# First attention of a block-sparse attention and FNet kernel: order written by hand, keys and queries turned two tokens at once, block sums on TensorE, a third value buffer

## Chip, cores, metric

The kernel runs on one core of one Trainium2 chip. The metric is device time in microseconds (us). The profile is that of one execution; its times count from the first instruction. Names of engines: PE is TensorE (PEld its weight loads), DVE is VectorE, ACT is ScalarE, POOL is GpSimd, SP is SyncE, which issues the transfers. PSUM is the memory that PE writes into, in banks of 512 fp32 columns on 128 partitions.

## What is computed

Four batches, eight heads, 768 tokens of 64 channels. Every query sees the keys closer than 16 tokens and, beside them, one summary for each of 24 blocks of 32 tokens: the maximum of the block's keys and the mean of its values. Then a mixing by Fourier transforms, a normalisation, and two dense layers (512 to 2048 to 512).

```python
k_sum = k.reshape(B, H, nb, block, D).max(axis=3)      # block = 32
v_sum = v.reshape(B, H, nb, block, D).mean(axis=3)
scores_l = scale * np.matmul(q, k.transpose(0, 1, 3, 2))
mask_l = np.abs(pos[:, None] - pos[None, :]) < window  # window = 16
scores_s = scale * np.einsum('bhsd,bhnd->bhsn', q, k_sum) + np.log(block)
...
out = np.matmul(softmax(concat(masked scores_l, scores_s)), concat(v, v_sum))
x = heads of out side by side, [B, S, 512]
u = x + np.real(fft(fft(x, axis=1), axis=2))
un = (u - mean(u)) / np.sqrt(var(u) + 1e-06)
result = u + np.maximum(un @ w_ch1, 0) @ w_ch2
```

Since exp(s + log 32) times a mean is exp(s) times a sum, the kernel works with block sums of the values.

## The kernel before

The program is one long pipeline. Attention of the next batch is interleaved with the dense layers of the current one, so that PE seldom rests; only batch 0's attention (the "first attention") has nothing to run beside, and it stands at the start. It is built differently from the others ("wide").

**The first attention** works on four pairs of heads, g = 0 to 3; a pair's two heads e = 0, 1 share the 128 partitions, 64 channels each. Its steps for a pair:

- `load` (L579) brings keys and queries, `kn` and `qn`, from memory with tokens on partitions, three tokens a partition. `prepare` (L703) turns them: 24 matmuls with the identity (L718), which the profile counts as 48 records, write channels onto partitions in PSUM (`qk`), and ACT copies (L719) bring them to `kt` and `qt`. `key_maxima` (L699, L700 on DVE) reduces `kt` to the 24 block maxima `km`.
- `wide_scores` (L740) takes queries in six blocks of 64, in two halves of three blocks. A block needs 96 keys (64 and 16 on each side). Local scores (L750) fill rows 0 to 95 of a score bank `sc`, the scores of the maxima (L754) rows 96 to 127. ACT takes exponentials (L756) into `p`, DVE multiplies by the mask `wide` (through the helper at L571).
- `block_sums` (L614) and `add_blocks` (L605): two transfers of 768 KB each bring the values of four heads once more, to the tile `words` as 96 blocks by 2048 numbers, and DVE adds halves five times (L571) to get the block sums `vbs`. `sum_values` (L762) spreads them with a selection matrix `sel` on PE (L767, into `vs`) and copies them to rows 96 to 127 of the value buffer `vw`, once for each query block (L769, DVE for pairs 0 and 3, ACT for 1 and 2).
- `load_values` (L664) brings the local values to rows 0 to 95 of `vw` in six transfers a pair; there are two such buffers, so pair 2 uses pair 0's after pair 0's values have been multiplied.
- `wide_values` (L772): PE multiplies (L777, into `av`), DVE takes reciprocals of the row sums (L781) and writes the products to `x`.
- `fold_sequence` and `fold_halves` (L896, L901) add and subtract halves of `x`, for the Fourier tables; each needs `x` of a pair, or of two.

**What sets the order.** For PE and DVE the order within `first_attention` is that of the code, under `tc.manual_schedule`; ACT's order there, and everything behind the first attention, is set by a list scheduler, which goes by ready times that it estimates and by priorities. SP issues its transfers in the order of the code (`fetch`, L549) up to the hidden layer. A few transfers can be outstanding at a time, so an SP instruction waits until a slot or a buffer is free, and those behind it wait as well.

**Behind the first attention** come the Fourier tables (PE lines 1258, 1262, 1297, 1299), the normalisation (DVE and ACT lines 1276 to 1331, then PE transposes at L1353), and the first hidden layer (`hx`, `hy`, `hz` at PE line 1381; the names are the seven-product scheme's banks, joined on DVE with `tt` into `h`). The attention of batch 1 runs beside them: its keys and queries are turned by 128x128 transposes (L726) and copied in pieces of 64 rows (L729). The weights arrive as 64-bit floats and are converted to fp32 on DVE and ACT on the way, in the lines 1092 to 1116 (`words` is the raw data, `w` the result); a conversion has two short DVE steps (0.7 us), three longer ones (1.2 us), and one or two of ACT.

## Time and profile before

| | us |
|---|---|
| median of three runs | 787.74 |
| lowest, highest | 786.42, 788.77 |
| profiled execution, span from first to last instruction | 787.6 |
| PE busy in that span | 771.0 (98%) |
| DVE busy | 536.3 (68%) |
| ACT busy | 241.8 (31%) |
| first scores of pair 0 (PE line 750) | 7.97 |
| last reciprocal of the first attention (L781, pair 3) | 43.77 |
| first hidden-layer matmul (PE line 1381) | 85.94 |

The span is the profiled execution's own time as the profile gives it. In the views, a row gives the start in us, the length, the engine, the line, the operation, what it writes and reads, and how many instructions the row groups; in brackets stands how long the engine was idle before, and what released it. Matmuls of one group may overlap, so that the distance between starts says more than lengths.

### The profile page before, as it was taken

The page shows a single profiled execution, that of the slowest core. Times are in us where ns is not written, and L with a number is a line of the kernel's source. Part 1 is how long each engine was busy: PE and PEld are TensorE (multiplying, and loading weights), DVE is VectorE, ACT ScalarE, POOL GpSimd, SP SyncE. Part 2 cuts the span into 40 slices and gives each one's busy share as a digit, 9 for nine tenths or more (in the row PEclk, how much of TensorE's full clock was granted, in tenths as well). Part 3 has the DMA queues.
Part 4 walks back from the last instruction along what each step waited for, and adds up shares of the span by engine and source line. Part 5 has one row for each costly group of instructions (what it writes and reads, how often), then busy time and mean ns, then how long its engine had stood idle before and what let it go on. Part 6 is the DMA issues. An engine that isn't in the chain of part 4 may idle for free.

```text
span 787.6 us, 14943 instructions
## 1 busy us (share of the span) xinstructions
PE 771.0 (98%) x6076; PEld 582.2 (74%) x6076; DVE 536.3 (68%) x1121; ACT 241.8 (31%) x561; POOL 74.6 (9%) x99
## 2 busy tenths in 40 slices
PE   8999899999999999999999999999999999999997
PEld 5878455445579866688569876688659889889986
DVE  4899979697988647652577635463476987766762
ACT  3555557236535112100226112210126214204300
POOL 0000000000000020200120011300030004201500
PEclk9999999999999999999999999999999999999999
DMA  8999785796966369996344159830614044204001
GB/s 182 200 279 236 178 281 158 232 251 230 222 196 177 71 174 189 261 156 143 123 185 141 54 172 180 210 109 10 253 48 158 27 164 170 94 1 188 1 28 57
DMA packets 133933, 121.87 MB, mean 155 GB/s; under 512 B 94528, under 2 KB 115232, under 8 KB 133664
## 3 DMA queue, kind: packets, MB, share of 16 engines
q1 hardware_dynamic: 132736, 118.53, 54.8%
q0 software_dynamic: 576, 2.10, 0.7%
q8 instruction: 50, 0.82, 0.5%
q10 hardware_dynamic: 544, 0.20, 0.1%
q14 instruction: 27, 0.22, 0.1%
HBM read 97.22 MB, written 23.59 MB: 153 GB/s over the span
## 4 chain that ended last, share of the span: by engine, by line
PE 86%; DVE 7%; ACT 3%; DMA 2%; issue 1%; SPq 0%; DVEq 0%
PE ox L1674 18%; PE hx L1381 15%; PE oz L1674 9%; PE hz L1381 7%; PE oy L1674 4%; PE t L1554 4%; PE o L1651 4%; PE hy L1381 4%; PE y L1258 3%; PE f L1554 2%; PE mx L1217 2%; PE sc L793 2%; PE av L829 2%; DMA words<-in_v_dram 1%; PE av L834 1%; PE ss L811 1%
## 5 line engine op out<-in xcount | busy, mean ns | idle before, releaser
L1381 PE MATMUL hx<-u,w 128*128 128x384 f32 x384 | 140.4, 494 | 1.3 <-ACT h L1398 0.8
L1381 PEld LDWEIGHTS hx<-u,w 128*128 128x128 f32 x384 | 70.9, 190 | 53.5 <-ACT p L800 3.7
L1674 PE MATMUL oz<-w,s 128*128 128x256 f32 x336 | 81.7, 380 | 0.0
L1674 PE MATMUL ox<-w,s 128*128 128x256 f32 x336 | 80.1, 380 | 0.0
L1674 PE MATMUL ox<-w,h 128*128 128x256 f32 x336 | 79.6, 381 | 0.0
L1674 PEld LDWEIGHTS ox<-w,h 128*128 128x128 f32 x336 | 63.0, 190 | 10.7 <-issue 1.2
L571 DVE TENSOR_TENSOR x<-ox,x 128x256 f32<-128x256 f32 x84 | 35.5, 423 | 51.2 <-PE ox L1674 50.8
L1381 PE MATMUL hz<-u,w 128*128 128x384 f32 x192 | 70.3, 487 | 0.0
L1674 PEld LDWEIGHTS ox<-w,s 128*128 128x128 f32 x336 | 63.0, 190 | 9.3 <-DVE s L571 0.4
L1674 PEld LDWEIGHTS oz<-w,s 128*128 128x128 f32 x336 | 63.3, 190 | 8.9 <-DVE x L571 0.4
L1381 PEld LDWEIGHTS hz<-u,w 128*128 128x128 f32 x192 | 36.3, 190 | 25.0
L1392 ACT COPY h<-hx 128x384 f32<-128x384 f32 x24 | 11.5, 479 | 119.6 <-PE hx L1381 119.6
L1651 PE MATMUL o<-w,h 128*128 128x512 f32 x96 | 42.3, 595 | 0.7 <-DVE w L571 0.7
L1674 PE MATMUL oy<-w,h 128*128 128x256 f32 x168 | 40.7, 381 | 0.7 <-ACT h L1603 0.7
L1557 ACT COPY f<-t 128x192 f32<-128x192 f32 x52 | 15.8, 303 | 78.3 <-PE t L1554 78.1
L1533 POOL TENSOR_SCALAR h<-h 128x768 f32<-128x768 f32 x12 | 25.4, 2127 | 137.5 <-DVE h L1513 137.5
L574 POOL TENSOR_TENSOR vb<-vb 96x512 f32<-96x512 f32 (+2 forms) x20 | 20.9, 1050 | 182.4 <-DMA vb<-in_v_dram 116.2
L571 DVE TENSOR_TENSOR x<-oz,x 128x256 f32<-128x256 f32 x42 | 17.8, 423 | 26.7 <-PE oz L1674 26.4
L1674 PEld LDWEIGHTS oy<-w,h 128*128 128x128 f32 x168 | 31.5, 190 | 5.9 <-ACT h L1603 1.5
L1381 PE MATMUL hy<-u,w 128*128 128x384 f32 x96 | 35.2, 488 | 0.0
L1651 PEld LDWEIGHTS o<-w,h 128*128 128x128 f32 x96 | 18.0, 190 | 22.7 <-issue 20.7
L571 DVE TENSOR_TENSOR h<-hy,h 128x384 f32<-128x384 f32 x24 | 13.4, 556 | 26.3 <-PE hy L1381 26.1
(222 smaller groups left out, 1328.8 us busy)
## 6 DMA issues: line engine op xcount, KB each, us to landing
w<-dw SPq DMA_DIRECT2D x42, 896.0 KB, 5.9
words<-in_moe_w_ch_dram SPq DMA_DIRECT2D x32, 512.0 KB, 5.9
dw<-w SPq DMA_DIRECT2D x12, 896.0 KB, 7.6
vw<-in_v_dram SPq DMA_DIRECT2D x47, 192.0 KB, 6.2
out_dram<-x SPq DMA_DIRECT2D x23, 256.0 KB, 2.0
vb<-in_v_dram SPq DMA_DIRECT2D x24, 192.0 KB, 7.2
kn<-in_k_dram SPq DMA_DIRECT2D x9, 384.0 KB, 6.2
qn<-in_q_dram SPq DMA_DIRECT2D x9, 384.0 KB, 7.3
```

Source lines behind the costliest of these rows:

```text
L571: return nc.vector.tensor_tensor(out=out, in0=in0, in1=in1, op=op).ins
L574: return nc.gpsimd.tensor_tensor(out=out, in0=in0, in1=in1, op=op).ins
L793: ins = nc.tensor.matmul(ps[h][r:r + 64, i, :], kt[rows, o:o + 64], qt[rows, o:o + BLOCK], start=True, stop=True)
L829: nc.tensor.matmul(av[r][32 * j:32 * (j + 1), t, :], p[rows, h, i - NB2 * h, :], vw[rows, i, :], start=(t == 0), stop=False, skip_group_ch ...
L1217: nc.tensor.matmul(out, y[:, g], table, start=False, stop=True, skip_group_check=True)
L1258: nc.tensor.matmul(y, fgs[b][par][:, st, P * g:P * (g + 1)], fs[par][:, g % 2, st, :], start=(st == 0), stop=(st == n - 1))
L1381: ins = nc.tensor.matmul(ps, w[:, a, kk, :], u[:, r, kk, :], start=start and kk == 0, stop=stop and kk == 1, skip_group_check=True)
L1533: nc.gpsimd.tensor_scalar(out=t, in0=t, scalar1=0.0, scalar2=None, op0=ALU.max)
L1554: marks["two"] = nc.tensor.matmul(o, left(j, a, m), rhs(r, m), start=m in (1, 5), stop=m in (2, 3, 4, 5, 7), skip_group_check=True).ins
L1557: nc.scalar.copy(out={1: f[:, 0], 6: f[:, 1], 7: g}[m], in_=t)
L1651: nc.tensor.matmul(ps, h[:, n, hf, P * t:P * (t + 1)], wt[2, b, j][:, 2 * hf:2 * hf + 2, :], start=(n, hf) == (0, 0), stop=(n, hf) == (NC ...
L1674: nc.tensor.matmul(ps, left[a][:, n, :], wt[2, b, j][:, r, :], start=start and n == 0, stop=stop and n == NC - 1, skip_group_check=True)
```

## The change

- **Turn.** `load` now brings batch 0's keys and queries as it does for batch 1, two tokens a partition. `turn` does 12 transposes of 128x128 a pair, three into each of four banks, and `place` copies each bank in two pieces of 64 rows, one token parity each. Pair 0's pieces go to ACT and DVE by halves; of the other pairs three banks go to ACT and one to DVE.
- **Block sums.** The two transfers of raw values, `add_blocks` and `sum_values` of batch 0 are gone. `add_parts` sums on PE: a new constant `blk` (64 KB, in place of the selection matrix in the first transfers) has ones over a block's 32 tokens; twelve matmuls a pair read the value buffer and write into the free columns 384 to 511 of a score bank, in four groups of 32 rows; ACT copies the result (128x128) to `words`. `spread_sums` is one matmul with `blk[:, 3]` into rows 96 to 127 of the same columns of another score bank, and two copies into the value buffer, head 0 on DVE and head 1 on ACT.
- **A third value buffer** `third`, in the tile that holds the mask, for pair 2; pair 3 uses pair 0's.
- **Order.** The loop over pairs is written out for PE, DVE and ACT; ACT is in the manual schedule as well. Pair g + 2 is turned between the two halves of pair g + 1's scores, and the values of a pair follow both halves of the next pair's scores. Some loads stand elsewhere in the code: `block_sums(1, 0)` and `load(1, 1)` earlier, `load_values(1, 0)` behind the first attention's last values, and `sel`, which batch 1 needs, behind the first attention.

Core of the diff:

```diff
-            if is_wide(b):
-                for h in range(2):
-                    ps = bank([P, S2], f"qk_{b}_{g}_{h}")
-                    for s in range(HT):
-                        for e in range(2):
-                            nc.tensor.matmul(ps[D * e:D * (e + 1), s:S2:HT], src[:, e, h, s, :], ident, start=True, stop=True)
-                    nc.scalar.copy(out=dst[:, S2 * h:S2 * (h + 1)], in_=ps)
...
+    def turn(g):
+        banks = {}
+        for n in (1, 0):
+            for e in range(2):
+                banks[n, e] = bank([P, S2], f"qk_0_{g}_{n}_{e}")
+                for j in range(NST // 2):
+                    nc.tensor.transpose(banks[n, e][:, P * j:P * (j + 1)], nat[0, g, n][:, e, j, :], ident)
...
+    def place(turned, n, e, copy):
+        banks, dst = turned
+        for s in range(2):
+            copy(out=dst[n][D * e:D * (e + 1), s:S:2], in_=banks[n, e][D * s:D * (s + 1)])
...
+    def add_parts(g, ps):
+        vw, ps = wide_vw(g), ps[:, S2:512].rearrange("p (e d) -> p e d", e=2)
+        for i in range(3):
+            for c in range(4):
+                nc.tensor.matmul(ps[32 * c:32 * (c + 1)], blk[0:WK, i], vw[0:WK, :, 3 * c + i, 0:D],
+                                 start=i == 0, stop=i == 2)
+        sums_of = words[:, 4096 + 2 * D * g:4096 + 2 * D * (g + 1)].rearrange("p (e d) -> p e d", e=2)
+        nc.scalar.copy(out=sums_of, in_=ps)
+        return sums_of
+    def spread_sums(g, sums_of, ps):
+        ps = ps[WK:P, S2:512].rearrange("p (e d) -> p e d", e=2)
+        nc.tensor.matmul(ps, blk[:, 3], sums_of, start=True, stop=True)
+        for e in range(2):
+            (nc.scalar.copy if e else nc.vector.tensor_copy)(
+                out=wide_vw(g)[WK:P, e, :, 0:D], in_=ps[:, None, e].to_broadcast([P - WK, NQ, D]))
...
+        for g in range(-1, NP - 1):
+            a, n = g + 1, g + 2
+            first, second = score_banks(a, 0), None
+            ps[a] = apool.tile([P, 2, NQ, QB], FP, tag="p", name=f"p_0_{a}")
+            if g >= 0:
+                spread[g] = add_parts(g, first[0])
+            wide_scores(a, 0, first)
+            exponentials(ps[a], 0, first)
+            masks(ps[a], 0)
+            if g >= 0:
+                spread_sums(g, spread[g], first[1])
+            second = score_banks(a, 1)
+            if n < NP:
+                turned = turn(n)
+                place(turned, 1, 0, nc.scalar.copy)
+                place(turned, 1, 1, nc.scalar.copy)
+                place(turned, 0, 1, nc.vector.tensor_copy)
+                key_maxima(n % 2)
+            else:
+                spread[n - 1] = add_parts(n - 1, second[0])
+            wide_scores(a, 1, second)
...
+            exponentials(ps[a], 1, second)
+            if n < NP:
+                place(turned, 0, 0, nc.scalar.copy) if g >= 0 else None
+            masks(ps[a], 1)
+            if n == NP:
+                spread_sums(n - 1, spread[n - 1], second[1])
+            if g >= 0:
+                wide_values(0, g, ps[g], x)
+            if g == 0:
+                load_values(0, 3)
+                load(1, 0)
+                get_tables(0, lambda: load_raw(1))
+                load_raw(2)
+                block_sums(1, 0)
+                load(1, 1)
+            for par in range(2 if g >= 0 else 0):
+                fold_sequence(par, g)
         fold_halves(0, 0)
-        wide_values(0, NP - 1, p[NP - 1], x)
+        wide_values(0, NP - 1, ps[NP - 1], x)
+        load_values(1, 0)
...
-    with tc.manual_schedule(engines={mybir.EngineType.PE, mybir.EngineType.DVE}):
+    with tc.manual_schedule(engines={mybir.EngineType.PE, mybir.EngineType.DVE, mybir.EngineType.Activation}):
         first_attention()
```

What this does to the order, at three places. First SP's transfers at the start; `kn_1` is the second pair's keys, `vw_84` the value buffer of pair 0, `words` the raw values. Before:

```order
L551 DMA kn_0_105<-in_k_dram 128x4x192
L551 DMA qn_0_107<-in_q_dram 128x4x192
L551 DMA kn_1_109<-in_k_dram 128x4x192
L551 DMA words<-in_v_dram 96x2048
L551 DMA qn_1_113<-in_q_dram 128x4x192
L551 DMA vw_84<-in_v_dram 96x10x64 x2
L551 DMA vw_84<-in_v_dram 80x64 x4
L551 DMA kn_2_174<-in_k_dram 128x4x192
L551 DMA qn_2_176<-in_q_dram 128x4x192
L551 DMA words<-in_v_dram 96x2048
```

and now:

```order
L562 DMA kn_0_105<-in_k_dram 128x6x128
L562 DMA qn_0_107<-in_q_dram 128x6x128
L562 DMA kn_1_109<-in_k_dram 128x6x128
L562 DMA qn_1_111<-in_q_dram 128x6x128
L562 DMA vw_84<-in_v_dram 96x10x64 x2
L562 DMA vw_84<-in_v_dram 80x64 x4
L562 DMA kn_2_173<-in_k_dram 128x6x128
L562 DMA qn_2_175<-in_q_dram 128x6x128
L562 DMA vw_85<-in_v_dram 96x10x64 x2
```

The second pair's queries and the values of pairs 0 and 1 move up by one place for each raw transfer that stood ahead of them.

Second, DVE at the end of the first attention, from the last key maxima on; `p_3` is pair 3's masks, `rec<-av_2` pair 2's reciprocals, `wide<-x` and `fold<-wide` the folds. Before:

```order
L700 TENSOR_REDUCE km_83<-kt_81 128x24
L571 TENSOR_TENSOR wide<-x_190 128x3x128 x2
L769 COPY vw_85<-vs_3_531 32x24x64
L571 TENSOR_TENSOR p_3_535<-p_3_535,wide 128x384 x2
L781 RECIPROCAL rec<-av_2_0_556 128x6
L571 TENSOR_TENSOR x_190<-av_2_0_556,rec 128x6x64
L781 RECIPROCAL rec<-av_2_1_557 128x6
L571 TENSOR_TENSOR x_190<-av_2_1_557,rec 128x6x64
L571 TENSOR_TENSOR wide<-x_190 128x3x128 x2
L571 TENSOR_TENSOR p_3_535<-p_3_535,wide 128x384 x2
L571 TENSOR_TENSOR fold_191<-wide 128x3x128 x2
L781 RECIPROCAL rec<-av_3_0_628 128x6
```

and now:

```order
L582 TENSOR_TENSOR wide<-x_145 128x3x128 x2
L582 TENSOR_TENSOR p_3_523<-p_3_523,wide 128x384 x2
L784 COPY wide<-sc_3_0_1_522 32x12x64
L582 TENSOR_TENSOR p_3_523<-p_3_523,wide 128x384 x2
L784 COPY vw_84<-sc_3_1_1_559 32x12x64
L796 RECIPROCAL rec<-av_2_0_594 128x6
L582 TENSOR_TENSOR x_145<-av_2_0_594,rec 128x6x64
L796 RECIPROCAL rec<-av_2_1_595 128x6
L582 TENSOR_TENSOR x_145<-av_2_1_595,rec 128x6x64
L582 TENSOR_TENSOR wide<-x_145 128x3x128 x2
L582 TENSOR_TENSOR fold_146<-wide 128x3x128 x2
L796 RECIPROCAL rec<-av_3_0_628 128x6
```

The second half of pair 3's masks moved ahead of pair 2's reciprocals, and one half-sized copy of block sums stands before, one behind it (`wide<-sc` writes the third value buffer, which lies in the mask's tile).

Third, DVE in the first hidden layer, from the products of batch 1's first pair on; `p_1` are masks and `km` key maxima of batch 1's second pair, `words` and `w` the conversion of weights, `h<-hy,h` the join of the first hidden block. Before:

```order
L571 TENSOR_TENSOR x_903<-av_0_1_1086,rec 128x2x3x64
L571 TENSOR_TENSOR p_1_1082<-p_1_1082,near 128x384
L1096 TENSOR_SCALAR words<-words 128x1024
L1109 TENSOR_SCALAR w_0_2_1026<-words 128x1024
L571 TENSOR_TENSOR p_1_1082<-p_1_1082,near 128x384
L700 TENSOR_REDUCE km_82<-kt_80 128x24
L1112 SCALAR_TENSOR_TENSOR words<-words 128x1024
L1114 SCALAR_TENSOR_TENSOR w_0_2_1026<-words,w_0_2_1026 128x1024
L571 TENSOR_TENSOR h_0_1244<-hy_0_1247,h_0_1244 128x384
L571 TENSOR_TENSOR w_0_2_1026<-w_0_2_1026,words 128x1024
```

and now:

```order
L1149 SCALAR_TENSOR_TENSOR words<-words 128x1024
L1151 SCALAR_TENSOR_TENSOR w_0_2_1032<-words,w_0_2_1032 128x1024
L1133 TENSOR_SCALAR words<-words 128x1024
L582 TENSOR_TENSOR w_0_2_1032<-w_0_2_1032,words 128x1024
L1146 TENSOR_SCALAR w_0_0_1182<-words 128x1024
L582 TENSOR_TENSOR w_0_2_1032<-w_0_2_1032 128x256
L1149 SCALAR_TENSOR_TENSOR words<-words 128x1024
L582 TENSOR_TENSOR w_0_2_1032<-w_0_2_1032 128x2x256
L1151 SCALAR_TENSOR_TENSOR w_0_0_1182<-words,w_0_0_1182 128x1024
L582 TENSOR_TENSOR w_0_2_1032<-w_0_2_1032 128x256
L582 TENSOR_TENSOR w_0_0_1182<-w_0_0_1182,words 128x1024
L582 TENSOR_TENSOR p_1_1088<-p_1_1088,near 128x384 x2
```

Now the rest of the conversion of `w_0_2` and all of the next, `w_0_0`, stand ahead of the masks, the maxima and the join, which follow these rows.

More of the change, by code (lines that the diff above doesn't have):

```diff
@@ new lines, in wide_scores, with exponentials, masks @@
+        for e in range(2):
+            rows = slice(D * e, D * (e + 1))
+            nc.tensor.matmul(banks[e][WK:P, 0:S2], km[rows, :], qt[rows, QB * n0:QB * n1], start=True, stop=True)
+    def exponentials(p, half, banks):
+        n0, n1 = NQ // 2 * half, NQ // 2 * (half + 1)
+        for e in range(2):
+            nc.scalar.activation(out=p[:, e, n0:n1], in_=banks[e][:, 0:S2].rearrange("p (n c) -> p n c", c=QB), func=AF.Exp,
+                                 scale=SC)
+    def masks(p, half):
+        n0, n1 = NQ // 2 * half, NQ // 2 * (half + 1)
+        for e in range(2):
+            tt(p[:, e, n0:n1], p[:, e, n0:n1], wide[:, None, :].to_broadcast([P, NQ // 2, QB]), ALU.mult)
```

134 lines of the change are left out of this document (48 added, 86 removed).

## The prediction

> **What bounds the kernel now.** First the page's busy shares and the table by windows, which cuts the first 134 us into stages: the first pair (4.6 to 16.6), pairs one to three (16.6 to 43.8), the mixing tables (43.8 to 60.6), the normalisation (60.6 to 86), the first hidden layer (86 to 134). Behind each engine stand its busy us, then the granted clock.
>
> ```profile
> span 787.6 us, 14943 instructions
> PE 771.0 (98%) x6076; PEld 582.2 (74%) x6076; DVE 536.3 (68%) x1121; ACT 241.8 (31%) x561; POOL 74.6 (9%) x99
> ...
> 16.60:43.80 27.20, 25.76 (x471) 20.25 (x469) 23.41 (x45) 12.18 (x23) 0.14 (x1) 1.00 0.90 210
> 43.80:60.60 16.80, 16.48 (x88) 13.87 (x88) 15.37 (x31) 11.08 (x32) 0.14 (x1) 1.00 1.16 264
> 60.60:86.00 25.40, 22.13 (x398) 17.58 (x397) 24.55 (x65) 12.80 (x24) 1.97 (x2) 0.96 1.04 225
> 86.00:134.00 48.00, 47.69 (x353) 27.56 (x353) 40.42 (x64) 30.40 (x58) 0.00 (x0) 0.99 0.69 205
> ```
>
> PE is busy nearly everywhere, so 98% says little; the stage in which the change works is read from the chain of waits over its first 140 us.
>
> ```profile
> 2.30 10.83 DMA words<-in_v_dram
> ...
> 81.27 2.54 issue
> ```
>
> The start waits for the raw values (`words`), and VectorE's adds of them come next. Both go with the change. VectorE (DVE) binds from 60.6 to 86 (24.55 of 25.40 us), PE afterwards. What the first attention saves is therefore carried through the tables and the normalisation; whether it is carried through the first hidden layer decides the result.
>
> **One pair of before, as a yardstick.** The timeline from pair one's exponentials to pair three's turn, ahead of it the program's first scores (start, length, engine, line, out<-in):
>
> ```profile
> 7.97 1.24 PE L750 MATMUL sc<-qt,kt 64*96 64x64 f32 x24
> ...
> 21.42 0.88 ACT L756 ACTIVATE p<-sc 128x384 f32<-128x384 f32 x2 [1.70 <-PE sc L754]
> ...
> 22.77 1.53 PE L718 MATMUL qk<-ident,kn 128*64 128x128 f32 x24
> ...
> 23.68 0.48 ACT L719 COPY kt<-qk 128x384 f32<-128x384 f32 x1 [1.39 <-PE qk L718]
> ...
> 24.08 1.53 PE L718 MATMUL qk<-ident,qn 128*64 128x128 f32 x24
> ...
> 24.91 0.95 DVE L700 TENSOR_REDUCE km<-kt 128x24 f32<-128x768 f32 x1 [0.41 <-ACT kt L719]
> ...
> 25.54 0.41 PE L767 MATMUL vs<-vbs,sel 96*32 96x64 f32 x4
> ...
> 25.88 1.24 PE L750 MATMUL sc<-qt,kt 64*96 64x64 f32 x24
> ...
> 27.05 0.84 PE L754 MATMUL sc<-qt,km 64*32 64x384 f32 x4
> 27.81 1.38 PE L750 MATMUL sc<-qt,kt 64*96 64x64 f32 x24
> ...
> 29.89 1.67 PE L777 MATMUL av<-vw,p 128*64 128x65 f32 x48
> ...
> 31.34 1.53 PE L718 MATMUL qk<-ident,kn 128*64 128x128 f32 x24
> ```
>
> Starts are surer than ends here, so I subtract starts. A pair takes 31.34 - 22.77 = 8.57 us: 1.31 for turning the keys, 1.46 for the queries with a wait, 0.34 for spreading the block sums, 1.17 for a half of the local scores and 0.76 for their maxima, 2.08 for the other half (27.81 to 29.89), 1.45 for the values.
>
> **The turn.** The new form, 128x128 transposes, already runs for batch 1, and so do its copies:
>
> ```profile
> 63.86 0.82 PE L726 MATMUL qk<-ident,kn 128*128 128x128 f32 x6
> ...
> 64.38 2.09 ACT L729 COPY kt<-qk 64x384 f32<-64x384 f32 x4 [4.19 <-PE qk L726]
> ...
> 64.51 0.82 PE L726 MATMUL qk<-ident,qn 128*128 128x128 f32 x6
> ...
> 82.83 1.28 DVE L1354 COPY u<-unt 128x512 f32<-128x512 f32 x2
> ```
>
> Six transposes take 64.51 - 63.86 = 0.65, so a pair's twelve take 1.31 instead of 2.62: PE gains 1.31. The copies grow: four of 0.48 (1.9 us on ScalarE, ACT) become eight of 0.52 (4.2). Six of the eight stay on ACT (3.1); two go to DVE. DVE's price for such a copy isn't in the trace; 0.64 for 512 columns gives 0.5 for 384 (between 0.48 and 0.64), so 1.0 a pair. ACT has room: it was busy 12.18 of 27.20.
>
> **The block sums.** What goes, and the copies into the value buffer:
>
> ```profile
> 13.16 2.72 DVE L571 TENSOR_TENSOR words<-words 96x1024 f32<-96x1024 f32 x4 [1.60 <-DMA words<-in_v_dram]
> ...
> 16.06 1.01 DVE L571 TENSOR_TENSOR p<-p,wide 128x384 f32<-128x384 f32 x2
> ...
> 17.96 1.76 DVE L769 COPY vw<-vs 32x1536 f32<-32x1536 f32 x1
> ```
>
> Adds of 16.06 - 13.16 = 2.9 us go twice, and the copies of the sums (1.76 on DVE for two pairs, ACT for the other two) are halved between both engines: 0.9 a pair on each. PE adds them up instead: 12 matmuls of 128 columns a pair, each two records, in four groups of 32 output rows. No run here shows such matmuls side by side in four groups. Row against row: eight score records in other tiles, and a full matmul with nothing beside it.
>
> ```profile
> 73.52 0.85 PE L811 MATMUL ss<-qt,km 64*32 64x384 f32 x8
> ...
> 74.30 0.43 PE L817 MATMUL vs<-vbs,sel 96*128 96x64 f32 x2
> ...
> 109.73 1.29 PE hx L1381 x4
> ```
>
> Alone, a record of 384 columns takes 1.29 / 4 = 0.32, one of 128 columns 0.107, and the 24 records 2.6 us: the upper end. The eight records of 73.52 took 0.78, 0.098 each where 0.32 would stand alone, a factor of 3.3; at that the sums take 0.8, and 0.65 at a factor of four. Before's four records in two groups (27.05) took 0.19 each, a factor of 1.7, which gives 1.5. I take 0.8, since four groups are what the change makes, and keep 0.65 to 2.6. The spread costs 0.25 (one matmul; before 0.34), the copy of the sums 0.3 on ACT. The Trainium skill's page "TensorE: Matmul & The Clock Gate", Part 3, lists 2.38 times for three column groups at 512 columns; by it alone the sums would take 2.6 / 2.38 = 1.1, an estimate from that page. That would delay the end by 1.2 us over the four pairs; no row of before can show it.
>
> **A pair of after.** PE: 1.31 + 2 x 1.17 + 2 x 0.76 + 1.45 + 0.8 + 0.25 = 7.7, against 8.57. DVE: copies 1.0, key maxima 0.95, masks 2 x 1.01, spread 0.9, reciprocals and products 1.5, fold 1.02: 7.4. So both engines are nearly full, and neither gains more than 0.9 a pair. ACT: 3.1 + 1.76 (four exponentials) + 0.3 + 0.9 = 6.1, no bound. The masks are 1.01 for two; the rest of these rows, and the end of before's attention:
>
> ```profile
> 39.36 0.20 DVE L781 RECIPROCAL rec<-av 128x6 f32<-128x6 f32 x1
> ...
> 40.88 1.03 DVE L571 TENSOR_TENSOR wide<-x 128x384 f32<-128x384 f32 x2
> ...
> 42.43 1.39 PE L777 MATMUL av<-vw,p 128*64 128x65 f32 x24 [0.56 <-DVE p L571]
> ...
> 43.77 0.20 DVE L781 RECIPROCAL rec<-av 128x6 f32<-128x6 f32 x1
> ```
>
> **The end of the first attention**, which is the last pair's reciprocal (43.77 before). First scores: 7.97 before, 8.5 with the longer copies shared by ACT and DVE. Pair zero: 8.5 + 1.17 + 0.76 + 1.31 + 1.17 + 0.76 = 13.7, half a microsecond of exponential, 1.01 of masks: 15.2. Three steps of DVE's 7.4, the last without copies and maxima (2.0), bring the last masks' end to 35.4. Behind them stand the spread 0.9, pair two's reciprocals and products 1.5 (39.36 to 40.88), and two folds of 1.02: 39.9, if DVE never waits. PE's pair is 0.3 longer than DVE's, thrice 0.3 is 0.9; and the last hand-over from engine to engine, with nothing beside it, 0.6 as at 42.43. I take 41.4, a gain of **2.4 us**. At worst all of DVE's idle time of before stays (27.20 - 23.41 = 3.8): 43.7, no gain; at best 3.9.
>
> **Up to the hidden layer.** The tables run on PE at 16.48 of 16.80: the gain passes. In the normalisation DVE binds. The block additions for batch 1 (`vb`) now come earlier and fill a wait in the weights' conversion, 0.75 at most; I take 0.5. Removing 1.57 MB of transfers is worth nothing more: pair zero's values, now ahead, are the transfer that takes over. Gain at the hidden layer's start: 2.9.
>
> ```profile
> 56.50 1.23 DVE L1112 SCALAR_TENSOR_TENSOR words<-words 128x1024 int32<-128x1024 int32 x1 [0.75 <-ACT words L1097]
> ...
> 95.68 1.24 DVE L1112 SCALAR_TENSOR_TENSOR words<-words 128x1024 int32<-128x1024 int32 x1 [1.58 <-ACT words L1097]
> ...
> 97.95 0.56 DVE L571 TENSOR_TENSOR h<-hy,h 128x384 f32<-128x384 f32 x1
> ...
> 99.55 0.70 DVE L1096 TENSOR_SCALAR words<-words 128x1024 int32<-128x1024 int32 x1
> ...
> 144.76 1.98 PE L1651 MATMUL o<-w,h 128*128 128x512 f32 x4 [0.71 <-DVE w L571]
> ```
>
> The chain has PE's next `hy` at
>
> ```profile
> 99.98 1.49 PE hy L1381 x4
> ```
>
> **In the hidden layer** the scheduler, with other ready times, puts two whole weight conversions ahead of the mask of pair one, the maxima and the join `h<-hy,h`; before, the join stood in the middle of the first (the third pair of orders above). The second conversion is 0.7 + 0.7 + 3 x 1.23 us, less some 0.1 of overlap each, 4.6; the rest of the first that now precedes the join is about 2.4 (one of 1.23 and three short steps); off go 1.2 for the two steps of 0.7 that before did there, and the wait for ACT behind them, 1.6 at 95.68. That leaves 4.2 us, and 5.4 if ACT holds each conversion up by 0.6: relative to the stage's start the join is that much later. PE has 1.5 us of slack there (the next block's `hy` starts at 99.98, the join ends at 98.5), and one group of four `hx` matmuls moved ahead of the waiting ones covers 1.5 more. The wait left is 1.2 to 2.4; I take **1.9**, with 0 and 2.4 as ends. Converted early, the second layer's first weights no longer hold PE at 144.76: 0.7 back (0 to 0.71). Sum: -2.4 - 0.5 + 1.9 - 0.7 = **-1.7**. Against the profiled span, 787.6 - 1.7 = 785.9; the span is 0.1 under the median of the runs, 787.74, so no correction is made. Behind 145 us PE binds, and I carry the shift to the end.
>
> **Rivals.** *The hidden layer gives nothing back*: the conversions are ready late anyway or PE has other matmuls; then 787.6 - 2.9 = 784.7, or 784.0 with the 0.7. For it: DVE was busy 40.42 of 48.00 in that stage and may catch up; against: the order is fixed, and the join stands behind 10 us of conversions.
>
> *The stall goes too.* PE waited 2.54 us on nothing shown at 81.27, and the granted clock then fell: the windows to 86 and to 134 stand at 0.96 and 0.99. That cost 2.5, and 25.4 x 0.04 + 48 x 0.01 = 1.5 of clock. Instructions now stand elsewhere, so it may go: 785.9 - 4.0 = 781.9.
>
> *Slower: the sums don't run side by side.* At 2.6 instead of 0.8, each of four pairs costs 1.8 more on PE, which then binds: 41.4 + 7.2 = 48.6, 4.8 behind before, and 4.8 - 0.5 + 1.9 - 0.7 = 5.5: 793.1. It decides from 0.8 + 1.7 / 4 = 1.2 us a pair on (no gain), and from 1.8 on it is slower than a measurement can miss. For it: each loads a tile of its own, and the four small ones at 25.54 took 0.34 for 64 columns each, no less than alone (4 x 0.107 / 2 = 0.21); against: 73.52.
>
> *Slower by the clock*: should PE's transposes let the clock fall as after 81.27, 1.5 us are lost each time, in three pairs 4.5: 785.9 + 4.5 = 790.4. The 12 transposes at 63.86 ran in windows with a clock of 1.00, beside other matmuls. The same page of the Trainium skill, Part 4, says that transposes do not count as PE work for the clock; the rows at 63.86 neither show nor exclude it.
>
> *Nothing gained*: the waits between the three hand-ordered engines keep the end at 43.7, and the hidden layer gives and takes little: 787.6.
>
> **Chances and numbers.** Forecast 785.9 (own range 784.9 to 787.5): 0.38. Hidden layer free: 0.26. Stall gone: 0.07. Nothing gained: 0.15. Sums not side by side 0.12, clock 0.02. About 0.3%, 2.4 us, is what a measurement can tell: under 785.4 lie the second and third cases and a quarter of the first (0.09), 0.42; over 790.1 the last two and 0.01 from the bounds, 0.15; between, 0.43. The range, 782.0 to 789.5, leaves out the slow cases and most of the stall's.
>
> **What would show it.** First scores at 8.5; twelve `sc<-vw` matmuls in 0.8; PE pairs 7.7 apart; the last reciprocal at 41.4 (41 to 43.7); the normalisation 2.9 earlier; the join `h<-hy,h` at 99.5 or later, with PE waiting for it for 1 to 2.4 us; no wait before the first `o<-w,h`. It is wrong if the last reciprocal is later than 43.7, if PE doesn't wait at the join, or if the time parts from the shift behind 145 us.

## The result, and the profile after

| | before | after |
|---|---|---|
| median of four runs beside each other, us | 788.25 (786.42 to 790.01) | 801.62 (799.74 to 803.22) |
| span of the profiled execution | 787.6 | 800.1 |
| last reciprocal of the first attention | 43.77 | 51.59 |
| first hidden-layer matmul | 85.94 | 89.71 |
| join of the first hidden block, `h<-hy,h` | 97.95 | 111.04 |

The changed kernel is slower: ratio 1.017 (95% interval 1.0147 to 1.0193). The forecast was 785.9 us with a range of 782.0 to 789.5; it is wrong in sign. The profiled execution's own time is 801.93; spans are compared with spans here, 12.5 us apart.

The page of after has the same shape as that of before, with 97% where 98% stood for PE:

```profile
span 800.1 us, 14854 instructions
PE 772.3 (97%) x6020; PEld 581.0 (73%) x6020; DVE 539.9 (67%) x1125; ACT 246.7 (31%) x573; POOL 75.1 (9%) x100
```

PE is busy 1.3 us more and the span is 12.5 longer, so the loss is waiting, and behind it a slower clock (a matmul at half clock counts as busy). The tables by windows of both kernels say where: first scores to last reciprocal of before, the same stretch of after, and after's first hidden layer (columns: window, length, busy us of PE, PEld, DVE, ACT, POOL, then the granted clock).

```profile
7.97:43.77 35.80, 32.93 (x579) 25.56 (x577) 27.99 (x52) 16.03 (x31) 0.14 (x1) 1.00 0.93 199
```

```profile
8.09:51.59 43.50, 35.78 (x559) 26.03 (x560) 27.62 (x52) 19.92 (x42) 0.28 (x2) 0.92 0.99 217
...
89.71:139.00 49.29, 42.83 (x321) 23.28 (x319) 46.62 (x69) 25.96 (x45) 0.00 (x0) 0.93 0.89 240
...
42.60:49.60 7.00, 6.05 (x87) 4.51 (x83) 3.33 (x7) 1.66 (x3) 0.00 (x0) 0.51 0.79 157
```

In the first attention PE is idle for 43.50 - 35.78 = 7.7 us, before 2.9; and for 6.8 us the clock stands at half. In the hidden layer it is idle for 6.5, before 0.3 (of 48.00), and 0.07 x 49.29 = 3.5 us of clock are gone, before 0.5. The sum of the spans: +7.8 to the last reciprocal, -4.05 from there to the first hidden matmul (38.12 us instead of 42.17: the wait of 2.54 us at 81.27 is gone, and with it the 3.41 us at half clock from 83.9), +8.8 from there to the end. That is 12.5.

**One pair of after**, from pair one's first scores to pair two's, and the start of pair three's:

```profile
15.27 0.27 ACT L776 COPY words<-sc 128x128 f32<-128x128 f32 x1
...
15.59 1.17 PEld L751 LDWEIGHTS sc<-qt,kt 64*96 64x96 f32 x24 [1.14 <-ACT words L776]
15.60 1.30 PE L751 MATMUL sc<-qt,kt 64*96 64x64 f32 x24 [0.86 <-DVE p L582]
...
16.83 0.83 PE L755 MATMUL sc<-qt,km 64*32 64x384 f32 x4
...
17.69 0.87 ACT L760 ACTIVATE p<-sc 128x384 f32<-128x384 f32 x2 [2.15 <-PE sc L755]
...
18.62 0.41 PE L782 MATMUL sc<-words,wide 128*32 128x128 f32 x2 [0.95 <-ACT p L760]
...
18.96 0.87 PE L731 MATMUL qk<-ident,kn 128*128 128x128 f32 x6
...
19.28 0.96 DVE L784 COPY vw<-sc 32x768 f32<-32x768 f32 x1
...
20.27 0.79 ACT L784 COPY vw<-sc 32x768 f32<-32x768 f32 x1 [1.71 <-DVE vw L784]
20.41 1.24 PE L751 MATMUL sc<-qt,kt 64*96 64x64 f32 x24
...
22.35 1.67 PE L792 MATMUL av<-vw,p 128*64 128x65 f32 x48
...
23.95 0.87 PE L773 MATMUL sc<-vw,wide 96*32 96x128 f32 x24
...
25.02 0.27 ACT L776 COPY words<-sc 128x128 f32<-128x128 f32 x1
...
25.34 1.30 PE L751 MATMUL sc<-qt,kt 64*96 64x64 f32 x24 [0.53 <-DVE rec L796]
...
35.13 1.30 PE L751 MATMUL sc<-qt,kt 64*96 64x64 f32 x24 [0.56 <-DVE rec L796]
```

A pair takes 25.34 - 15.60 = 9.74 us. The matmuls go as forecast: the twelve of the sums 0.87 side by side, the turn 20.41 - 18.96 = 1.45. What is new are three hand-overs. The sums stand in columns 384 to 511 of the bank that the next pair's scores are about to fill in columns 0 to 383, and PE starts these only when ACT has read the sums out (15.27 + 0.27 = 15.54, scores at 15.60; the matmuls' row names `p`, but the weight load ahead of them, at 15.59, names ACT's copy to `words`, and so it does for the next two pairs). The spread is to go beside the scores of the second bank, and waits until ACT has read those (17.69 + 0.87 = 18.56, spread at 18.62). And the two copies of the spread, one on DVE and one on ACT, out of one bank, go one after the other (19.28, then 20.27). No column is shared in any of the three; the bank is.

Over the whole first attention the groups of PE show it: the scores of before, then scores and spread of after, with the idle time ahead of them and its releasers behind the bar.

```profile
L750 PE MATMUL sc<-qt,kt 64*96 64x64 f32 x192 | 10.5, 249 | 0.3 <-ACT p L756 0.3
```

```profile
L751 PE MATMUL sc<-qt,kt 64*96 64x64 f32 x192 | 10.5, 249 | 4.7 <-ACT words L776 1.9 <-DVE rec L796 1.1 <-DVE p L582 0.9
...
L782 PE MATMUL sc<-words,wide 128*32 128x128 f32 x8 | 1.9, 319 | 3.8 <-ACT p L760 3.8
```

Here 8.5 us stand where 0.3 stood. The longest wait, 1.87 us, stands in the last pair, where there is no turn for PE to do:

```profile
39.09 0.96 DVE L784 COPY wide<-sc 32x768 f32<-32x768 f32 x1 [0.31 <-issue]
...
40.08 0.79 ACT L784 COPY wide<-sc 32x768 f32<-32x768 f32 x1 [1.99 <-DVE wide L784]
40.90 0.27 ACT L776 COPY words<-sc 128x128 f32<-128x128 f32 x1
...
41.22 1.30 PE L751 MATMUL sc<-qt,kt 64*96 64x64 f32 x24 [1.87 <-ACT words L776]
...
51.59 0.19 DVE L796 RECIPROCAL rec<-av 128x6 f32<-128x6 f32 x1
```

ACT's copy of the spread waits for DVE's, the copy of the last pair's sums stands behind it on ACT, and PE's last scores behind that.

The Trainium skill's page "PSUM — Partial Sum Buffer", section "PSUM bank collisions raise a hardware error", has a rule that fits this: accesses of two engines to the same bank and the same 32 partitions have to be kept apart by semaphores, whatever the columns. The waits agree with it; the exponentials read all 128 rows and the spread writes rows 96 to 127, so by that rule other rows were no way out; no run tried them.

**The hidden layer of after**, timeline: the first hidden matmul, the first and the last of the long conversion steps that stand ahead of the join on DVE (the order in the change's third list), the mask, and the join.

```profile
89.71 0.81 PE L1418 MATMUL hx<-u,w 128*128 128x384 f32 x2
...
99.96 1.22 DVE L1149 SCALAR_TENSOR_TENSOR words<-words 128x1024 int32<-128x1024 int32 x1
...
108.10 1.23 DVE L582 TENSOR_TENSOR w<-w,words 128x1024 f32<-128x1024 f32 x1
109.24 1.03 DVE L582 TENSOR_TENSOR p<-p,near 128x384 f32<-128x384 f32 x2
...
109.90 0.79 PE L844 MATMUL av<-vw,p 64*32 64x65 f32 x50 [3.39 <-issue]
...
111.04 0.56 DVE L582 TENSOR_TENSOR h<-hy,h 128x384 f32<-128x384 f32 x1
...
111.65 1.65 PE L1418 MATMUL hy<-u,w 128*128 128x384 f32 x2 [0.96 <-DVE h L582]
```

The join comes 21.33 us behind the first hidden matmul, before 12.01. PE waits 3.39 us and then 0.96 for the join, and from 111.0 the clock is at half for 6.83 us. The row of the 3.39 names no releaser; it is read here as a wait for the mask, since these matmuls read `p` and start at 109.90, just behind the first of the two masks (109.24 + 1.03 / 2 = 109.8).

### The profile page after: what moved, and what is told of

The parts are those of the page before. It is cut to its first block, busy times and chain, and to the rows that moved or that the text cites. A ratio compares the mean times of both kernels' runs of the same rounds, so it can differ in the third digit from the quotient of the medians.

```text
span 800.1 us, 14854 instructions
## 1 busy us (share of the span) xinstructions
PE 772.3 (97%) x6020; PEld 581.0 (73%) x6020; DVE 539.9 (67%) x1125; ACT 246.7 (31%) x573; POOL 75.1 (9%) x100
## 4 chain that ended last, share of the span: by engine, by line
PE 84%; DVE 10%; ACT 3%; issue 1%; DMA 1%; SPq 0%; DVEq 0%; ACTq 0%
PE ox L1711 17%; PE hx L1418 14%; PE oz L1711 9%; PE hz L1418 7%; PE o L1688 5%; PE oy L1711 4%; PE t L1591 4%; PE hy L1418 4%; PE y L1295 3%; PE f L1591 2%; PE mx L1254 2%; PE sc L808 2%; DVE w L582 2%; PE av L844 1%; PE av L849 1%; DVE p L582 1%
## 5 line engine op out<-in xcount | busy, mean ns | idle before, releaser
L1429 ACT COPY h<-hx 128x384 f32<-128x384 f32 x24 | 11.5, 478 | 124.7 <-PE hx L1418 124.7
L1448 ACT ACTIVATE h<-hx 128x384 f32<-128x384 f32 x24 | 11.7, 489 | 63.1 <-PE hx L1418 63.1
```

Of the source, the lines that this page charges most:

```text
L1448: nc.scalar.activation(out=c21, in_=X, func=AF.Relu)
```

## The experiments

For the first attention the theory was the **bank**: the sums share score banks, and the engines wait for each other's use of a bank. Its rival was **ACT's order**: written out by hand, it makes ACT late. For the hidden layer the theory was that the scheduler's order of two conversions on DVE is the loss, whatever the first attention does. Measured times are medians; the ratio is to runs of before on the same chip.

**1. A bank of its own for the sums** (and one for the last pair's, not shown).

```diff
-                spread[g] = add_parts(g, first[0])
+                own = bank([P, 512], f"own_{g}")
+                spread[g] = add_parts(g, own)
...
-                spread_sums(g, spread[g], first[1])
+                spread_sums(g, spread[g], own)
```

> The block sums get a PSUM bank of their own from the pool that the turn uses; every engine's order stays as in the changed kernel. Theory A (the sums share the score banks, so scores wait for ACT's copy of the sums, 0.5 to 0.9 us, and the spread, with the turn queued behind it, waits for the exponentials, 0.95): both waits go, a pair falls from 9.76 to 8.0 to 8.6 us, the wait of 1.87 at 41.22 goes, the last reciprocal comes at 43 to 46 instead of 51.6, the half clock from 42.7 on does not occur, total 793 to 796. Theory B (ACT's order written by hand delivers keys, queries and sums late; the bank matters little): pair at least 9.3, last reciprocal after 49, total within 2 us of 801.6.

Measured: 801.16, ratio 1.0156 (1.0105 to 1.0206): no gain, which by its numbers is the rival's outcome; run 2 takes the rival up. Two of the three waits are gone from where they stood, and a new one stands at the turn. Timeline:

```profile
15.05 1.24 PE L751 MATMUL sc<-qt,kt 64*96 64x64 f32 x24
...
18.66 0.96 DVE L784 COPY vw<-own 32x768 f32<-32x768 f32 x1
...
19.66 0.79 ACT L784 COPY vw<-own 32x768 f32<-32x768 f32 x1 [1.71 <-DVE vw L784]
...
20.50 0.56 PE L731 MATMUL qk<-ident,qn 128*128 128x128 f32 x3 [1.99 <-ACT vw L784]
```

The scores no longer wait (15.05, straight behind the sums), nor does the spread for the exponentials; ACT's copy still waits for DVE's, out of one bank (1.71). But the banks go round: the turn's fourth bank is the one that the sums just had, and PE waits 1.99 us until both copies have read it, twice. A bank more, without an earlier release, moved a good part of the wait. The clock did the rest: it was at half for 6.83 us in the first of the two pairs and for 3.41 in the second, and they took 13.27 and 11.81. Less half of that time, an estimate, they take 9.9 and 10.1, no less than after's 9.74, and the last reciprocal, at 51.71, would be at about 46.6, as the last pair no longer waits 1.87.

**2. ACT's order left to the scheduler.**

```diff
-    with tc.manual_schedule(engines={mybir.EngineType.PE, mybir.EngineType.DVE, mybir.EngineType.Activation}):
+    with tc.manual_schedule(engines={mybir.EngineType.PE, mybir.EngineType.DVE}):
```

> ACT is taken out of the manual schedule, as it was before; PE and DVE keep the changed kernel's order. Theory A: pair still 9.5 to 9.9, last reciprocal 50.5 to 52.5, total 800 to 803. Theory B: pair 8.8 or less, last reciprocal before 48, total under 798.

Measured: 801.79, ratio 1.016 (1.0112 to 1.0207). ACT now copies three pieces of the keys ahead of the sums; a pair takes 9.64. The spread waits 3.8 us in all as in after, the scores 4.4 instead of 4.7. The last reciprocal is at 49.26, earlier than expected, with the clock whole (49.66 for after's order at whole clock, run 11). The theory of ACT's order falls.

**3. The sums left out** of the changed kernel, and their rows in the value buffers set to zero.

```diff
-                spread[g] = add_parts(g, first[0])
...
-                spread_sums(g, spread[g], first[1])
...
+        nc.gpsimd.memset(wide_vw(g)[WK:P, :, :, 0:D], 0.0)
```

> The first attention's block sums are left out: no summing matmuls, no spread, no copies; the rows for them in the value buffers are set to zero once (so the block part of batch 0's attention is missing). Turn, order and third buffer stay. Theory A: without the sums nothing of the new order waits, a pair takes 6.7 to 7.3, the last reciprocal comes at 38 to 41. Theory C (the turn's new form and its longer copies make the pair long): pair at least 8.5, last reciprocal after 45. The order that the scheduler gives DVE in the first hidden layer is another one here, with the join early: by the theory of the hidden layer PE does not wait there and the clock stays whole, total 780 to 785.

Measured: 782.63, ratio 0.9922 (0.9895 to 0.9949). The scores of pairs one to three:

```profile
15.88 1.30 PE L751 MATMUL sc<-qt,kt 64*96 64x64 f32 x24
...
23.22 1.30 PE L751 MATMUL sc<-qt,kt 64*96 64x64 f32 x24 [0.27 <-DVE rec L796]
...
30.54 1.30 PE L751 MATMUL sc<-qt,kt 64*96 64x64 f32 x24 [0.26 <-DVE rec L796]
```

A pair takes 7.33; the last reciprocal is at 39.56. So the sums cost 9.74 - 7.33 = 2.4 us a pair, of which their matmuls are 0.87 + 0.33, half. The rest is hand-overs and copies.

**4. One conversion released later.** The plan's entry for the second layer's first weights waits for the first hidden block:

```diff
-(2, 0, ("mx", 0))
+(2, 0, ("h", 0, 0))
```

> One number of the weights' plan: the conversion of the second layer's first weights is released by the first hidden block instead of by the mixing, so it no longer stands ahead of the join on DVE (4.6 us of DVE with its waits). The first attention is untouched: last reciprocal 51.6 as before. Theory H (the order in the hidden layer makes PE wait, 3.4 us and 1 us, and the clock halves behind it): join 4.5 to 6 us earlier relative to the layer's first matmul (21.3 now), PE's wait of 3.39 gone, no half clock behind 110, total 793 to 796.5. Rival H2 (late data, since the late first attention has shifted the transfers of weights): the join stays 19 us or more behind the layer's first matmul, total within 2 us of 801.6.

Measured: 796.53 (ten runs), ratio 1.0091 (1.0067 to 1.0116). From the first hidden matmul to the join 17.3 us instead of 21.3, a little less than expected, and from the first hidden matmul to the end of the span 705.2 instead of 710.4: 5.3 back before rounding. PE's wait of 3.39 and the half clock behind it are gone. The first attention is that of after, and yet its last reciprocal is at 55.87 here, as the clock was at half for 17.1 us.

**5. Sums early**: a bank of its own, the sums right behind the pair's own second scores, the spread ahead of the next pair's scores.

```diff
             if g >= 0:
-                spread[g] = add_parts(g, first[0])
+                spread_sums(g, spread[g], own)
             wide_scores(a, 0, first)
...
             exponentials(ps[a], 1, second)
+            if n < NP:
+                own = bank([P, 512], f"own_{a}")
+                spread[a] = add_parts(a, own)
```

> The block sums again have a bank of their own, but now they are added right behind the pair's second scores, before the next pair's turn needs that bank, and are spread ahead of the next pair's scores; for the last pair they are added between its two halves. Nothing else changes; the order in the first hidden layer stays the bad one. Theory A: neither scores, nor spread, nor turn wait for another engine's reading of their bank, so a pair is the 7.34 us without sums plus 0.87 and 0.25 of PE, less the 0.3 that PE waits there anyway: 7.7 to 8.3; last reciprocal 42 to 45, and 2 to 3.4 later if the clock halves once; total 793 to 797. Rival B (the sums cost what they cost wherever they stand, since ACT and DVE are full): pair 9.2 or more, total 799 or more.

Measured: 794.33, ratio 1.0083 (1.0062 to 1.0103); pairs of 8.05 and 9.32; last reciprocal at 45.07, 4.6 ahead of the same stretch of after at whole clock (run 11). The pair of 9.32 shows what is left:

```profile
27.70 0.79 ACT L784 COPY vw<-own 32x768 f32<-32x768 f32 x1 [3.88 <-DVE vw L784]
...
28.55 0.55 PE L731 MATMUL qk<-ident,qn 128*128 128x128 f32 x3 [1.04 <-ACT vw L784]
```

ACT waits for DVE's copy, which stands behind reciprocals and a fold, and PE's turn for ACT's. The hidden layer still loses (first hidden matmul to end 708.7).

**6. The spread behind the turn on PE**, in the shared bank.

```diff
-            if g >= 0:
-                spread_sums(g, spread[g], first[1])
             second = score_banks(a, 1)
             if n < NP:
                 turned = turn(n)
+            if g >= 0:
+                spread_sums(g, spread[g], first[1])
+            if n < NP:
```

> Only the order of PE changes: the spread and its copies stand behind the next pair's turn instead of ahead of it; the banks are shared as in the changed kernel. Theory A: the spread's wait for the exponentials (0.95) is covered by the turn, the wait of the scores for the copy of the sums stays; pair 8.7 to 9.2, last reciprocal 47 to 50, total 798 to 801. Rival B: pair 9.6 or more.

Measured: 803.18, ratio 1.0214 (1.0176 to 1.0253), and pairs of 10.03, 0.3 longer than after's: a miss. Timeline:

```profile
19.47 0.41 PE L782 MATMUL sc<-words,wide 128*32 128x128 f32 x2
...
20.91 0.79 ACT L784 COPY vw<-sc 32x768 f32<-32x768 f32 x1 [1.93 <-DVE vw L784]
...
24.42 0.96 PE L773 MATMUL sc<-vw,wide 96*32 96x128 f32 x24 [1.01 <-ACT p L760]
```

The spread of this pair doesn't wait any more, but, counted from the pair's first scores (16.01 here, 15.60 in after), it comes 0.44 later and ACT's copy 0.23 later, and behind that stand ACT's copies of the keys and the exponentials: now the next sums wait for those, 1.01 us. Taking one wait away by delay gave it to the next in the ring.

**7. Run 5 with both conversions released later** (the entry of 4, and that of `w_0_2`).

```diff
-(1, 2, ("mx", 0))
+(1, 2, ("h", 0, 0))
```

> The block sums as in the kernel with the early sums, and two numbers of the weights' plan: the conversions of the first layer's third weights and of the second layer's first are released by the first hidden block. Theories A and H together: last reciprocal 42 to 45; the join 12 to 14 us behind the hidden layer's first matmul (before 12.0, changed kernel 21.3); no wait of PE there beyond 1 us unless the third weights come late; total 785 to 790, so no slower than before. If H is wrong and the gap behind the hidden layer's start is made by late transfers, 793 or more.

Measured: 785.36 (784.14 to 787.77, ten runs), ratio 0.996 (0.9944 to 0.9977): faster than before by 0.4%, an interval that leaves out 1. Join 10.9 us behind the first hidden matmul; last reciprocal 44.40; the clock whole in the first attention and the hidden layer.

**8. The two heads' spreads in two banks**, the rest as in after.

```diff
-        nc.tensor.matmul(ps, blk[:, 3], sums_of, start=True, stop=True)
+        for e in range(2):
+            nc.tensor.matmul(ps[e], blk[:, 3], sums_of[:, e], start=True, stop=True)
```

> The spread of the two heads goes to two score banks (two matmuls) instead of one, so that DVE and ACT copy from different banks; all else as in the changed kernel. Theory A (two engines that read one bank are made to take turns): ACT's copy no longer starts behind DVE's (now always 1.0 us behind); at the end of the first attention, where ACT's copy of the last sums and with it PE stand behind that, PE's wait of 1.87 falls to about 1; in the steady pairs little changes, 9.5 to 9.8. Last reciprocal 0.5 to 1.5 earlier at the same clock, total 800 to 802. Rival (ACT's copy waits because both write one buffer): no change.

Measured: 796.76, ratio 1.0119 (1.0095 to 1.0143); better than the low end expected, 5.3 us of span under after. Of these, rounded, 2.0 are the edit's in the first attention (last reciprocal 47.66, against 49.66 of after's order at whole clock, run 11), 1.9 are after's half clock there, which did not occur, and 1.3 lie behind the first hidden matmul, where the clock was at half for 3.41 us instead of 6.83. Pairs of 9.52. The copies into the same buffer now run together:

```profile
18.98 0.79 ACT L785 COPY vw<-sc 32x768 f32<-32x768 f32 x1 [0.39 <-PE sc L783]
...
19.30 0.97 DVE L785 COPY vw<-sc 32x768 f32<-32x768 f32 x1
```

So it was the bank that they read, not the buffer that they write, that put them in turn. The scores' and the spread's waits stay, but shorter: 2.9 and 2.6 us in all instead of 4.7 and 3.8. The spread now waits 0.57 each time, as its first matmul writes into the bank whose scores ACT reads first; the last pair's scores wait 0.39 instead of 1.87.

**9. Run 7 with both copies of the spread on ACT.**

```diff
-            (nc.scalar.copy if e else nc.vector.tensor_copy)(
+            nc.scalar.copy(
```

> As the kernel with the early sums and the two late conversions, with both copies of the spread sums on ACT, so that they no longer stand behind DVE's reciprocals and folds (in that kernel ACT waited 3.9 us for DVE's copy of the same bank, and PE 1.0 us for ACT's at the turn's last bank). Theory A: every steady pair takes 7.6 to 8.2 (there 8.05 and 9.32), last reciprocal 42 to 43.5 (there 44.4), total 782 to 785. Rival B (ACT is the bound once it has all copies): pair 8.6 or more, total as there, 785.4, or more.

Measured: 784.94 (782.84 to 789.22, twelve runs), ratio 0.9957 (0.9939 to 0.9975), level with run 7. Both pairs take 8.05, as expected:

```profile
18.79 1.24 PE L751 MATMUL sc<-qt,kt 64*96 64x64 f32 x24
...
26.84 1.24 PE L751 MATMUL sc<-qt,kt 64*96 64x64 f32 x24
26.95 1.49 ACT L784 COPY vw<-own 32x768 f32<-32x768 f32 x2 [0.66 <-PE own L782]
...
34.90 1.24 PE L751 MATMUL sc<-qt,kt 64*96 64x64 f32 x24
```

One engine alone reads the bank; two copies take 1.49 there, and the two in turn of after (19.28 to 20.27 + 0.79) 1.78. The last reciprocal is nevertheless at 45.19, later than the 42 to 43.5 expected, since pair one starts at 18.79 instead of 16.00 (run 7): the clock was at half from 8.7 to 15.5.

**10. Before, with the two later conversions.** The edits of 4 and 7 in the kernel before.

> The kernel before, with the two conversions released by the first hidden block; first attention untouched. Theory H: in the kernel before, the join already stood early on DVE and PE did not wait there, so nothing is to be gained: join 10.5 to 12 us behind the hidden layer's first matmul (12.0), total 786 to 790. Rival: the mended kernel's gain lies in the plan alone; then 785.5 or less.

Measured: 792.49, ratio 1.0063 (1.0048 to 1.0078): slower, and over what was expected. The join is early (8.4 us), but the first `o<-w` stands 52.1 us behind the first hidden matmul instead of 45.7; its weights are released later. From the first hidden matmul to 185 us PE waits 3.1 us, before 1.0, and the clock is at half for 3.41 us from 124.7. So the gain of 7 and 9 over before is not owed to the plan alone.

**11. After, with the two later conversions.** The same edits in the changed kernel.

> The changed kernel with both conversions released by the first hidden block; its first attention untouched. Theory H: join 11.5 to 14 us behind the hidden layer's first matmul (21.3), no wait of PE over 1 us there, no half clock in the hidden layer; first attention as in the changed kernel (last reciprocal 49.3, or 51.6 and more if the clock halves); total 791.5 to 795.5. Rival H2 (late data): 797 or more.

Measured: 794.62, ratio 1.0089 (1.0072 to 1.0106). The clock stayed whole, with the same waits in the first attention:

```profile
8.08:49.66 41.58, 33.40 (x559) 24.19 (x560) 27.68 (x52) 19.89 (x42) 0.28 (x2) 1.00 0.98 225
```

PE is idle for 8.2 us against 2.9, and busy for 33.4 against 32.9. That is the first attention's loss without the clock: 5.9 us at the last reciprocal. Hidden layer:

```profile
87.79 0.81 PE L1418 MATMUL hx<-u,w 128*128 128x384 f32 x2
...
99.20 0.55 DVE L582 TENSOR_TENSOR h<-hy,h 128x384 f32<-128x384 f32 x1
```

The join is 11.4 us behind the first hidden matmul, and after's 8.8 us are gone but for 1.2 (first hidden matmul to end 702.85, before 701.64).

**12. Before, without its sums** (the two transfers, the adds and the spread left out, their rows set to zero).

```diff
-                sum_values(0, g + 1)
...
-    block_sums(0, 0)
-    block_sums(0, 1)
```

> The kernel before without batch 0's block sums: no transfers of raw values, no adds on DVE, no selection, no copies; rows set to zero once (the block part of batch 0's attention is missing). It tells what the turn and the order are worth by themselves, beside the changed kernel without sums (pair 7.34, last reciprocal 39.56 with the clock halved for 3.4 us). Theory A: they are worth 0.5 to 1.2 us a pair: pair 7.9 to 8.6, last reciprocal 39.5 to 42, total 782 to 787. Rival D (the turn and the order gain nothing): pair 7.5 or less, last reciprocal 38.5 or earlier.

Measured: 784.50 (ten runs), ratio 0.9954 (0.9935 to 0.9972); pairs of 8.12 and the last reciprocal at 38.71, at whole clock. Against run 3: turn and order save 8.12 - 7.33 = 0.8 us a pair, but the last reciprocal comes no earlier (39.56, some of it by 3.41 us at half clock). The old sums cost 43.77 - 38.71 = 5.1 us there; the new ones 49.66 - 39.56 = 10.1 (run 11 against run 3), and about 1.7 more if run 3's lapse of the clock hadn't been.

## Why the prediction was wrong

- **The parts on PE were right.** First scores 8.09 (8.5). Sums side by side 0.87 (0.8, with ends 0.65 and 2.6; the other estimate, 1.1, was too long). Spread 0.34 (0.25). Turn 1.45 (1.31).
- **The step that failed is "A pair of after"**, and with it "I take 41.4". It added up each engine's work, PE 7.7 and DVE 7.4, and let one hand-over of 0.6 stand for all waits. The pair took 9.74. The sums had been put into the score banks, which closes a ring: scores wait for ACT to copy the sums, the spread for ACT's exponentials, ACT's copy for DVE's, and ACT's next copies for that. Run 3 prices ring and matmuls together at 2.4 us a pair, runs 1 and 8 show the bank at work, run 5 gets 4.6 us back by breaking the ring. Nothing in before warned of it in the rows, but the diff did: `first[0]` and `first[1]` are handed to `add_parts` and `spread_sums`, and each such bank has three users.
- **The upper end, 43.7, was no bound.** It let all idle time of DVE in before stay, 3.8 us; in after PE alone waits 8.2 (run 11). Idle time of before says nothing about waits that the change makes. The last reciprocal's +7.8 is 5.9 of this and 1.9 of clock: the same stretch ended at 49.66, 51.59 and 55.87 with 0, 6.8 and 17.1 us at half clock (runs 11, after, 4).
- **The rival of the sums that don't run side by side** had the right place and sign, 48.6, by the wrong mechanism: they do run side by side, so that its nearness to 49.66 (run 11) is luck.
- **"Gain at the hidden layer's start: 2.9"** was a loss of 3.8. The rival that the stall at 81.27 goes too was given 0.07, and it did go. From the normalisation's first transposes (71.97 before, 80.14 now) to the first hidden matmul it is 9.57 us instead of 13.97: 4.4 shorter, priced at 4.0 with its clock, part of that behind this stretch. The 0.5 for the block additions doesn't show: from the last reciprocal to those transposes it is 28.55, before 28.20.
- **The hidden layer's mechanism was right, its size was not.** Measured from the same transposes the join is 30.90 behind instead of 25.98: 4.9 later, forecast 4.2 to 5.4. But the forecast gave PE 3 us of slack and a wait of 1.9; without the stall PE was 4 us nearer to DVE, and waited 3.39 + 0.96 (2.0 more in four smaller waits), and behind that the clock fell, 3.4 us. So the second term that failed is the 1.9 for this wait: with the 0.7 given back the forecast had 1.2 there, and 8.8 were measured. Two terms had been priced as if each were alone, and the clock behind the wait at nothing. The 0.7 itself came: no `o<-w,h` up to 165 us waits now. Run 11 undoes the loss by the two plan entries.
- **"Behind 145 us PE binds, and I carry the shift"** holds nearly: the last of the 96 `o` matmuls starts at 191.7 instead of 179.6, 12.1 later, the end is 12.5 later.

What stays open: why PE waited 2.54 us at 81.27 in before. The kernels with the change show waits of at most 1.3 us of that kind; run 12 lacks the stall too, and run 10 has 1.8 us that end at 77.0 (and the clock at half for 3.41 us from there). No run took its cause away by itself, but the traces have a candidate: at 81.27, just as the wait begins, a load of 16 KB of instructions starts (one packet on the queue q8, kind "instruction", 1.2 us), and the wait ends 2.54 us behind that start. From 8 us on, the timelines of before and of the kernels here put thirteen waits of PE over 0.25 us down to "issue", the 3.4 at the mask left aside, and each ends 2.3 to 3.1 us behind the start of such a load (run 10's 3.07). So PE may have waited for its instructions; that is not shown.

Of what run 9 gains over before (3.3 us of span), 3.8 come between the last reciprocal and the first hidden matmul, where the stall is absent, and 0.9 behind the first hidden matmul, while 1.4 are still lost at the last reciprocal: the first attention, mended, is about as long as before's (0.6 later in run 7), not shorter.

## What to carry to other kernels

Count a PSUM bank as one lock: list who writes and reads it in order, and price every change of hands (PE waited 0.5 to 1 us at most of them here, 2.0 at worst) before taking free columns of a bank in use; a spare bank helps only if its last reader is done before the pool hands it out again. Where two engines copy out of one bank, give them two banks or the job to one engine. And when a change moves ready times, look at what the scheduler puts ahead of the next join on each engine, and price that with and without the slack that other terms of the sum take away.

## What was not expected of the hardware

- **The clock halves after much shorter waits than 3.4 us.** It fell at 42.7 in after, behind waits of 0.95 and 1.87 us, for 6.83; in run 4, with the same waits, at 43.3 for 10.24, and before that at 9.2 for 6.83, behind waits of 0.73 and 0.76; in run 11, with the same first attention, not at all. The Trainium skill's page "TensorE: Matmul & The Clock Gate", section "HAM oscillation — how this bites in real kernels", puts the limit at idle gaps of over about 3.4 us; these rows don't agree with it as a limit, but they do come in multiples of 3.41 us and the same first attention has them in one execution and not in another. It ended 1.9 and 6.2 us later for them: what one execution shows of a stage full of waits of 1 to 2 us is uncertain by that much.
- **Four column groups of 32 run three times as fast as one after the other**: 24 records of 128 columns in 0.87 us, where 0.107 each would be 2.6. That is near the factor of 3.3 that the forecast took from another tile shape.
- **Two engines that copied out of one bank took turns in this program**: ACT waited 1.71 to 1.99 us for DVE; out of two banks they ran together (run 8). The releasers in the views come from semaphores, so this is how the program guards a bank; what the chip would do without them no run shows.
